# A spectral filter and the feed-forward block that gates it, on one core: one interleaved order of emission, statistics on two engines, filter rows gathered late

## The chip, the cores and the metric

One NeuronCore of one Trainium2 chip. The metric is the device time of one execution in microseconds (us), as the median of several executions. All runs here are of programs on one core; a run counts as "slow" when it is over 1.5% above the fastest run of the same kernel, and comparisons use the others alone.

Engines are named as the profile names them: PE is TensorE's matmul unit (PEld its weight loads), DVE is VectorE, ACT is ScalarE, POOL is GpSimd, SP is SyncE. A "q" behind the name (ACTq, SPq) marks the engine's own work of issuing DMAs. The "granted clock" is the share of PE's full clock that the profile records as let through. Its record starts only with PE's first dense work; for earlier windows the views print 1.00 without a record.

## The reference, cut to what matters

```python
def reference(A_x, A_w_r, A_w_i, B_x, B_w_gate, B_w_up, B_w_down):
    x  = A_x                                   # (1, 2048, 640) bf16
    xn = layernorm(x)                          # over the 640 columns, eps 1e-5
    s  = irfft2(rfft2(xn) * (w_r + 1j*w_i))    # over 2048 x 640; the filter has 2048 x 321 entries
    g  = silu((gelu(xn @ w_gate) * (xn @ w_up)) @ w_down)      # 640 -> 1536 -> 640
    return x + s * g
```

The two branches, spectral filter and feed-forward, need only `xn` and meet only in the last line. Both Fourier transforms are done as matmuls with constant tables.

## The kernel before

The kernel cuts the 2048 rows into 16 slabs of 128 and emits its work in blocks: loads and all 32 gathers of filter rows; statistics, normalisation and first Fourier stage ("fold") of all slabs; the whole spectral chain for eight groups G; then, for each of four groups of slabs, 12 gate/up steps followed by four times (inverse transform, down projection, result). The framework's scheduler can take later instructions forward, as far as buffers allow. The parts that matter, with cuts marked:

```python
    for G in range(8):                                   # 32 gathers, first thing on GpSimd
        for pm in range(2):
            for ri, wsrc in enumerate((A_w_r, A_w_i)):
                nc.gpsimd.indirect_dma_start(out=Wt[:, G, pm, ri, 0:L], ...)
    # ... loads of BD, Wd, I1T, IM, IT on GpSimd as well

    for b in range(4):
        for j in range(4):                               # statistics: VectorE only
            # ... bn_stats twice, bn_aggr -> mva[:, j]
        nc.gpsimd.tensor_scalar_add(out=ve, in0=mva[:, :, 1], scalar1=1e-5)
        nc.gpsimd.tensor_tensor(out=rstd, in0=ve, in1=mh, op=ALU.pow)
        for j in range(4):
            nc.vector.tensor_scalar(out=xn, in0=X[:, n1, :], scalar1=mva[:, j, 0:1], scalar2=rstd[:, j:j + 1], ...)
            nc.sync.dma_start(out=xnD[n1 * P:(n1 + 1) * P, :], in_=xn)             # to DRAM ...
            nc.sync.dma_start_transpose(out=xnT[...], in_=xnD[...])                # ... and back, transposed
        for j in range(4):                               # fold
            # ... eo, xf on VectorE; pa on TensorE
            A = work.tile([P, D], BF16, tag="s4", name=f"A{n1}", bufs=3)
            nc.scalar.copy(out=A, in_=flat(pa)[:, 0:D])
            nc.sync.dma_start(out=D2[:, n1, :], in_=A)   # regrouping goes through DRAM
    for q in range(4):
        nc.sync.dma_start(out=Bv[:, 4 * q:4 * q + 4, :], in_=D2[...])

    for G in range(8):                                   # the spectral chain
        # ... pzt (for every fourth G), pz -> Z -> pe -> E -> V -> M, N, Y, R (VectorE) -> pi -> IU
        nc.sync.dma_start(out=D3[G]..., in_=IU...)
    # ... reload of D3 into Uv

    for grp in range(4):                                 # feed-forward and inverse
        for t in range(12):
            # ... pg (5 matmuls), pu (5 matmuls), ge = gelu(pg) on ScalarE
            u = work.tile([P, 512], BF16, tag="uT", name=f"uT{grp}_{t}", bufs=14)
            nc.vector.tensor_tensor(out=u, in0=pu, in1=ge, op=ALU.mult)
        for j in range(4):
            y = inverse(n1)                              # pv, Vt, py, ... needs the whole chain
            # ... ph (24 matmuls), tanh, gating, result
```

## Time and profile before

| | before |
|---|---|
| median time (three runs) | 347.28 us |
| span of the profiled run | 345.6 us |
| PE busy | 224.3 us (65%) |
| first gate/up matmul (`pg`) | 60.7 us |
| spectral chain on PE, first `pzt` to last `pi` | 96.8 to 185.5 us |
| first inverse (`pv`) / first down projection (`ph`) | 193.5 / 196.2 us |

The first lines come from the page of the kernel before: busy time by engine, then the busy share in 40 equal slices of the span, in tenths (each slice is 8.6 us here).

```profile
PE 224.3 (65%) x1328; PEld 124.5 (36%) x1328; DVE 154.1 (45%) x366; ACT 101.1 (29%) x148; POOL 41.2 (12%) x50
...
PE   0000012958589983644352587999999999999873
...
POOL 6777791000000000000000000000000000000000
PEclk9999999998969998766665589999999999999999
```

PE is dense only from slice 26 on. It does next to nothing for seven slices, is patchy to slice 12, and patchy again, at a lower granted clock, from slice 16 to 24. The windows of the same run give these stretches in numbers (columns: window, its length, then for each engine busy us with the number of instructions; last the granted clock of PE, the DMA share and GB/s):

```profile
0.00:52.00 52.00, 1.21 (x4) 0.46 (x4) 18.42 (x65) 1.98 (x2) 40.42 (x50) 1.00 0.83 271
52.00:100.00 48.00, 30.35 (x130) 12.85 (x129) 22.41 (x73) 16.96 (x26) 0.77 (x1) 0.91 0.75 209
...
125.00:195.00 70.00, 30.93 (x184) 18.08 (x181) 30.02 (x54) 21.08 (x26) 0.00 (x0) 0.70 0.15 55
195.00:343.00 148.00, 138.04 (x875) 80.81 (x875) 68.65 (x146) 49.67 (x79) 0.00 (x0) 0.98 0.12 38
```

Two stretches lose the most: 52 us at the start with 1.2 us of PE work, and 70 us in the middle with 30.9. What happens in the first is in the timeline of the kernel before (start, duration, engine, instruction; in brackets the idle time of that engine just before, and what ended it):

```profile
24.64 0.21 DVE L234 BATCH_NORM_AGGREGATE mva_406<-stats_419 128x2 f32<-128x12 f32 x1
...
42.13 0.95 POOL L214 DMA_INDIRECT Wt<-in_A_w_i_dram,LANE  x1 [0.30 <-issue]
...
46.67 1.09 POOL L238 TENSOR_TENSOR rstd_169<-ve_168,mh 128x4 f32<-128x4 f32 x1
...
47.80 0.45 DVE L243 TENSOR_SCALAR xn_172<-X,mva_151,rstd_169 128x640 bf16<-128x640 bf16 x1 [22.95 <-POOL rstd_169 L238]
```

VectorE has all statistics at 24.9 us. GpSimd is still issuing gathers, one every 1.25 us, the last at 42.1, and computes the first `rstd` only at 46.7. VectorE stands still for 22.95 us. PE's waits show this and what the middle stretch waits for:

```profile
PE pa_194 L259 <- DVE xf_191 L256: 50.5, 1, 50.5
PE pv_1161 L355 <- DMA BU<-D_93: 8.1, 1, 8.1
PE pg_0_967 L388 <- DMA xnT<-xnD: 6.5, 1, 6.5
...
PE pi_0_785 L337 <- DVE R_781 L326: 5.1, 1, 5.1
```

A line like the last one comes for five of the eight G: PE gives VectorE the spectrum and waits 4.9 to 5.1 us for the filtered one (`R`). In that stretch there is no feed-forward work to put in: the next down projection stands behind an inverse that needs the whole chain, and the gate/up steps have used the 14 `u` buffers.

### The profile page before, as it was taken

How to read it: one execution, taken by the hardware profiler on the slowest of the kernel's cores; microseconds unless marked ns; L12 is line 12 of the kernel's file. 1: busy time of each engine (PE TensorE's matmuls, PEld its weight loads, DVE VectorE, ACT ScalarE, POOL GpSimd, SP SyncE). 2: the span in 40 equal slices, each digit the busy share in tenths (PEclk: the TensorE clock that was granted, in tenths of full speed). 3: DMA queues.
4: the chain of work that ended last, by engine and by line, in shares of the span. 5: the costliest groups of instructions: out<-in, count | busy, mean ns of one | idle time of the engine just before them, and what ended most of it. 6: DMA issues, size and time to landing. Idle time of an engine off the chain costs nothing. (4 is left out here: it accounts for less than half of the span.)

```text
span 345.6 us, 3623 instructions
## 1 busy us (share of the span) xinstructions
PE 224.3 (65%) x1328; PEld 124.5 (36%) x1328; DVE 154.1 (45%) x366; ACT 101.1 (29%) x148; POOL 41.2 (12%) x50
## 2 busy tenths in 40 slices
PE   0000012958589983644352587999999999999873
PEld 0000000423244442322231355546654466544652
DVE  2580046583207644354533136634563345633453
ACT  0000003433233553422330124233422334223341
POOL 6777791000000000000000000000000000000000
PEclk9999999998969998766665589999999999999999
DMA  7999286778570111101111811200220001200011
GB/s 268 372 339 310 67 269 174 226 218 193 142 275 1 41 38 38 39 4 35 38 38 38 307 38 38 78 0 22 57 78 0 1 23 55 65 13 0 21 39 38
DMA packets 33745, 34.85 MB, mean 101 GB/s; under 512 B 13168, under 2 KB 31344, under 8 KB 33600
## 3 DMA queue, kind: packets, MB, share of 16 engines
q1 hardware_dynamic: 25840, 23.67, 21.9%
q0 software_dynamic: 2208, 6.01, 5.3%
q10 hardware_dynamic: 5680, 4.95, 4.7%
q8 instruction: 10, 0.16, 0.2%
q14 instruction: 7, 0.06, 0.1%
HBM read 21.50 MB, written 10.50 MB: 93 GB/s over the span
## 5 line engine op out<-in xcount | busy, mean ns | idle before, releaser
L388 PEld LDWEIGHTS <-Wg 128*128 128x128 bf16 x240 | 23.4, 100 | 33.1 <-issue 8.7
L391 PEld LDWEIGHTS <-Wu 128*128 128x128 bf16 x240 | 23.9, 101 | 28.1 <-issue 3.5
L259 PE MATMUL pa_194<-xf_191,F1T 128*128 128x512 bf16 x1 | 0.6, 584 | 50.5 <-DVE xf_191 L256 50.5
L337 PEld LDWEIGHTS <-BD 128*128 128x128 bf16 x64 | 7.3, 124 | 35.0 <-DVE R_781 L326 5.3
L260 PEld LDWEIGHTS <-F1T 128*128 128x128 bf16 x16 | 1.7, 104 | 44.3 <-issue 43.9
L214 POOL DMA_INDIRECT Wt<-in_A_w_r_dram,LANE x16 | 15.2, 952 | 5.8 <-issue 4.6
L214 POOL DMA_INDIRECT Wt<-in_A_w_i_dram,LANE x16 | 15.1, 946 | 4.9 <-issue 4.9
L243 DVE TENSOR_SCALAR xn_172<-X,mva_151,rstd_169 128x640 bf16<-128x640 bf16 x1 | 0.4, 446 | 22.9 <-POOL rstd_169 L238 22.9
L262 ACT ACT_TABLE_LOAD x1 | 1.3, 1283 | 25.5 <-DMA Wu<-in_B_w_up_dram 25.5
L355 PEld LDWEIGHTS <-BU 128*128 128x128 bf16 x64 | 5.0, 100 | 10.3 <-DMA BU<-D_93 8.7
L259 PEld LDWEIGHTS <-F1T 128*128 128x128 bf16 x16 | 1.7, 108 | 18.1 <-DMA F1T<-tab_f 12.0
L262 ACT CAST A_197<-pa_194 128x640 bf16<-128x640 f32 x1 | 0.7, 692 | 24.5 <-PE pa_194 L260 24.5
L289 PEld LDWEIGHTS <-BU 128*128 128x128 bf16 x64 | 5.9, 125 | 2.3 <-issue 1.3
L388 PE MATMUL pg_0_967<-xnT,Wg 128*128 128x512 bf16 x5 | 2.3, 625 | 6.5 <-DMA xnT<-xnD 6.5
L355 PE MATMUL pv_1161<-I1T,BU 128*128 128x128 bf16 x4 | 0.6, 308 | 8.1 <-DMA BU<-D_93 8.1
L396 DVE TENSOR_TENSOR uT_8_1109<-pu_8_1096,ge_8_1107 128x512 bf16<-128x512 f32 x1 | 0.7, 692 | 10.0 <-PE pu_8_1096 L391 10.0
L374 DVE TENSOR_TENSOR y_1179<-y_1177 128x320 bf16<-128x320 bf16 x1 | 0.3, 326 | 10.9 <-ACT y_1177 L371 10.9
L280 PE MATMUL pzt_496<-T_77,BU 128*128 128x128 bf16 x8 | 1.2, 311 | 5.2 <-DMA BU<-D_92 5.2
L337 PE MATMUL pi_0_895<-R_891,BD 128*128 128x322 bf16 x4 | 1.3, 469 | 5.1 <-DVE R_891 L326 5.1
L337 PE MATMUL pi_0_785<-R_781,BD 128*128 128x322 bf16 x4 | 1.3, 468 | 5.1 <-DVE R_781 L326 5.1
L337 PE MATMUL pi_0_950<-R_946,BD 128*128 128x322 bf16 x4 | 1.3, 468 | 5.1 <-DVE R_946 L326 5.1
L337 PE MATMUL pi_0_719<-R_715,BD 128*128 128x322 bf16 x4 | 1.3, 469 | 5.0 <-DVE R_715 L326 5.0
(1054 smaller groups left out, 633.5 us busy)
## 6 DMA issues: line engine op xcount, KB each, us to landing
BU<-D_93 SPq DMA_DIRECT2D x4, 644.0 KB, 6.0
BU<-D_92 SPq DMA_DIRECT2D x4, 640.0 KB, 6.2
Wg<-in_B_w_gate_dram ACTq DMA_DIRECT2D x4, 480.0 KB, 15.0
Wu<-in_B_w_up_dram ACTq DMA_DIRECT2D x4, 480.0 KB, 13.0
X<-in_A_x_dram SPq DMA_DIRECT2D x3, 640.0 KB, 11.6
Wd<-in_B_w_down_dram POOLq DMA_DIRECT2D x1, 1920.0 KB, 9.1
BD<-tab_bd POOLq DMA_DIRECT2D x1, 1024.0 KB, 9.3
X<-in_A_x_dram SPq DMA_DIRECT2D x2, 320.0 KB, 6.8
```

What stands on the lines that cost most here:

```text
L214: nc.gpsimd.indirect_dma_start(out=Wt[:, G, pm, ri, 0:L], out_offset=None, in_=wsrc, in_offset=bass.IndirectOffsetOnAxis(ap=LANE[:, 2 * G ...
L243: nc.vector.tensor_scalar(out=xn, in0=X[:, n1, :], scalar1=mva[:, j, 0:1], scalar2=rstd[:, j:j + 1], op0=ALU.subtract, op1=ALU.mult)
L259: nc.tensor.matmul(pa[:, 0, :], lhsT=F1T, rhs=xf[:, :, 0:128], start=True, stop=True)
L260: nc.tensor.matmul(pa[:, 1, 0:128], lhsT=F1T, rhs=xf[:, :, 128:160], start=True, stop=True)
L262: nc.scalar.copy(out=A, in_=flat(pa)[:, 0:D])
L280: nc.tensor.matmul(pzv[:, i, :, h, :], lhsT=Bv[:, g, 512:640], rhs=T2[:, g, :], start=True, stop=True, skip_group_check=True)
L289: nc.tensor.matmul(pzv[:, c, :, h, :], lhsT=Bv[:, g, c * P:c * P + P], rhs=T2[:, g, :], start=True, stop=True, skip_group_check=True)
L337: nc.tensor.matmul(pi[:, pq, 0:LP], lhsT=BD[:, G, ro, ri, :], rhs=R[:, ri, pq, :], start=(ri == 0), stop=(ri == 1))
L355: nc.tensor.matmul(pvf[:, c * P:c * P + P], lhsT=U[:, cols[c]], rhs=I1T, start=True, stop=True, skip_group_check=True)
L388: nc.tensor.matmul(pg, lhsT=Wg[:, c, t * P:(t + 1) * P], rhs=xnT[:, c, q0:q0 + 512], start=(c == 0), stop=(c == 4))
L391: nc.tensor.matmul(pu, lhsT=Wu[:, c, t * P:(t + 1) * P], rhs=xnT[:, c, q0:q0 + 512], start=(c == 0), stop=(c == 4))
L396: nc.vector.tensor_tensor(out=u, in0=pu, in1=ge, op=ALU.mult)
```

## The change

Its intent: the work is emitted in one list of 64 feed-forward steps (48 gate/up steps, 16 down projections), and each piece of the rest is hung behind one step, so the spectral chain always has feed-forward matmuls between its pieces. A down projection no longer stands behind an inverse; nine `G2` buffers hold its result, and `u` has 16 buffers instead of 14. Statistics go to VectorE for one slab in three and to ScalarE for two; the transposed `xn` comes from PE for the first four slabs and by DMA straight from SBUF for the rest; the gathers are spread; the table of activation functions is loaded at the start.

```diff
-    for G in range(8):
-        ... 32 gathers, then BD, Wd, I1T, IM, IT on GpSimd
+    nc.scalar.activation(out=warm, in_=warm, func=ACT.Gelu_apprx_tanh)      # table load first
     ... X on SyncE (six pieces instead of five)
     for q in range(4):
         nc.scalar.dma_start(out=Wg[:, :, cs], in_=gv[:, :, cs])
         nc.scalar.dma_start(out=Wu[:, :, cs], in_=uv[:, :, cs])
+    nc.scalar.dma_start(out=Wd, ...)
+    for t, k in ((T2, "t2"), (FM, "fm"), (FT, "ft"), (BD, "bd"), (I1T, "i1"), (IM, "im"), (IT, "it")):
+        nc.scalar.dma_start(out=flat(t), in_=tabs[k])
...
+    def norm(n1):
+        if n1 % 3 == 0:
+            ... bn_stats, bn_aggr on VectorE, + eps on GpSimd
+        else:
+            nc.scalar.activation(out=junk, in_=x, func=ACT.Copy, scale=-1.0 / D, accum_out=nm)
+            nc.scalar.activation(out=junk, in_=x, func=ACT.Square, bias=nm, accum_out=ss)
+            ... mean, variance + eps on GpSimd
+        nc.gpsimd.tensor_tensor(out=rstd, in0=rstd, in1=mh, op=ALU.pow)
+        ... xn on VectorE
+        if n1 < 4:
+            ... five nc.tensor.transpose, then nc.scalar.copy(out=xnT[...], in_=pt)
+        else:
+            nc.sync.dma_start_transpose(out=xnT[:, :, n1 * P:(n1 + 1) * P], in_=xn)
...
+    def gather(G):
+        W = buf("W", "W", 4, (P, 2, 2, LP))
...
+    ffn = []
+    for grp in range(4):
+        ffn += [(gate_up, grp, t) for t in range(12)] + [(down, 4 * grp + j) for j in range(4)]
+    after = {i: [] for i in range(64)}
+    for i in range(12):
+        after[i].append((norm, 4 + i))
+        ... fold(nf), four of them for every three steps
+        if i in (5, 7, 9, 11):
+            after[i].append((gather, (i - 5) // 2))
+    after[11].append((regroup,))
+    for G in range(8):
+        i = 14 + 2 * G
+        after[i].append((spectral_a, G))
+        after[i + 1].append((spectral_b, G))
+        if G < 4:
+            after[i + 1].append((gather, G + 4))
+    after[29].append((reload,))
+    ... inverse(n1) at 32 + 2 * n1, final(n1) one step later
+    for i, (fn, *a) in enumerate(ffn):
+        fn(*a)
+        for f2, *b in after[i]:
+            f2(*b)
```

## The prediction

> **What bounds the kernel now.** TensorE, but only for part of the span: busy 224.3 of 345.6 us (page, part 1). Three stretches waste it.
>
> 1. 0 to 50.5 us: nothing on PE but a weight load (timeline). VectorE has its statistics by 24.9 us, then waits 22.9 us for rstd (costliest groups), because GpSimd first issues 32 filter gathers at 1.25 us each, up to 43 us. The first gate/up matmul starts only at 60.7 us, behind the xnD round trip through DRAM.
> 2. 52 to 100 us: PE is 15.7 of 28, then 14.6 of 20 us busy (windows).
> 3. 125 to 195 us: PE 30.9 of 70 us, granted clock 0.70. The feed-forward order has run out: 14 u buffers, and the first down projection stands behind the inverse. The spectral chain runs alone, about 10.7 us per G (pz to pz at 142.2, 153.4, 164.1), with 5.1 us of PE waiting for R each time.
>
> From 195 us on PE is dense (138 of 148 us, clock 0.98), so little can be gained there.
>
> **What the change does.** Statistics of slabs 1, 2, 4, 5... go to ScalarE (two passes of about 0.7 us, an estimate from the 128x640 casts); gathers of later G come late; the first four slabs are transposed on PE (20 small matmuls), the other twelve by DMA straight from SBUF, so the xnD write and wait go. Down projections no longer wait for the spectral chain: the instruction order puts about 26 feed-forward matmuls into each G. The table load moves to the start.
>
> **Costs, in order.**
> - ScalarE now issues 16 DMAs before its first computation, and the last one waits for the last Wu chunk. Before, all of X and W had landed by about 27 us; I count 8.4 MB ahead of it at about 340 GB/s, so ScalarE is free at about 25 us. "DMA: Bandwidth & Descriptors" of the Trainium skill (Issuing engines are not separate DMA queues) says queues share the same 16 engines; the trace agrees (DMA share 0.99 in 0 to 30 us). GpSimd still has 16 gathers in front, to about 24 us. Then statistics of slabs 1 and 2, pow (1.1 us), xn, transposes, copies: first gate/up matmul at about 33 us (was 60.7).
> - Group 0 (12 gate/up, 12 norms, 16 folds): 30 us of warm PE work, but VectorE and ScalarE each have about 31 us in it too: about 40 us.
> - The whole matmul order is 197 us at 2.4 GHz (estimate: columns/2.4 plus 2.5 ns, "TensorE: Matmul & The Clock Gate", Wait; the trace has 1.08 us for 5x512, which agrees).
> - Spectral stretch: chain 9.7 to 10.7 us per G against 8.9 us of PE: about 8 us of stalls. Reload: 8 us against 7 us of fill.
> - Later bubbles 4 us, tail 5 us.
>
> 33 + 196 + 10 + 8 + 1 + 4 + 5 = about 258 us. Some 27 us come from the start, the rest from filling 125 to 195 us.
>
> **Signs.** First gate/up at 30 to 36 us; no 22.9 us rstd wait; one table load; PE over 80% busy at clock near 1.0 from 80 us on; waits for R under 2 us; PE total about 225 us or less.
>
> **What would make it wrong.** SBUF-sourced DMA transposes could occupy the SP queue far longer than the 1.21 us of the DRAM-sourced ones; D2 stores queue behind them and everything slides. ScalarE freed later than 25 us. GpSimd's small operations (1.6 us per slab) or shared buffers serialising group 0. Then 280 us or more.
>
> Predicted 258 us, 8 in 10 between 243 and 284. Faster 0.95, same 0.02, slower 0.03.

## The result, and the profile after

The changed kernel takes 262.26 us (median of 4 runs, 261.18 to 263.19) against 347.41 us for the kernel before in the same rounds. The ratio is 0.7551, with a 95% interval from 0.7509 to 0.7593. Ratios here and below are the mean time of one kernel's fast runs over the mean of the other's fast runs of the same rounds, so they are not quite the ratio of the medians quoted.

The page of the kernel after (a slice is 6.5 us now):

```profile
PE 208.8 (80%) x1348; PEld 118.2 (45%) x1348; DVE 144.5 (56%) x337; ACT 117.5 (45%) x192; POOL 50.2 (19%) x87
...
PE   0010079999999999999999877779999999999881
```

PE has 15.5 us less busy time than before although it has 20 matmuls more (its mean granted clock is 0.995 against 0.914), and it is dense from slice 7 on; slices 23 to 27 are the only soft spot. The windows, cut at the stages:

```profile
0.00:36.00 36.00, 2.91 (x21) 2.03 (x22) 10.49 (x33) 8.78 (x18) 21.33 (x38) 1.00 1.01 333
36.00:68.00 32.00, 31.63 (x150) 14.26 (x149) 25.03 (x79) 26.92 (x56) 12.88 (x30) 1.00 0.61 165
68.00:78.00 10.00, 10.00 (x75) 7.16 (x74) 2.33 (x3) 2.10 (x3) 0.00 (x0) 1.00 0.62 211
78.00:166.00 88.00, 79.34 (x515) 43.85 (x514) 53.56 (x97) 41.92 (x57) 15.95 (x20) 1.00 0.17 51
166.00:174.00 8.00, 6.59 (x50) 4.44 (x48) 3.09 (x5) 2.60 (x4) 0.00 (x0) 1.00 0.55 185
174.00:255.00 81.00, 78.32 (x546) 46.43 (x543) 48.22 (x119) 35.14 (x55) 0.00 (x0) 1.00 0.23 76
```

The spectral chain (78 to 166 us) takes about as long as before (87.3 us, 88.7 before), but PE is now busy 79.3 of its 88 us at full clock. Of 51.1 us without PE work (259.9 less 208.8), 33.1 lie in the first 36 us. The timeline of the kernel after shows the start:

```profile
27.31 0.95 POOL L282 DMA_INDIRECT W<-in_A_w_i_dram,LANE  x1 [0.30 <-issue]
28.11 0.69 ACT L245 COPY xnT<-pt 128x640 bf16<-128x640 bf16 x1 [25.37 <-issue]
...
31.45 0.45 DVE L240 TENSOR_SCALAR xn<-X,mean,rstd 128x640 bf16<-128x640 bf16 x1 [15.48 <-POOL rstd L238]
```

Only half of "gathered late" came about: the pool `W` has four buffers, so the scheduler took the first 16 gathers forward to 7.5 to 28.3 us, and only the other 16 are late. ScalarE does its first work on data at 28.1 us, 25.4 us after the small activation that brings the table load, because it was issuing loads: 17.0 of the 25.4 us are issues, the rest lies between them. VectorE still waits for `rstd`, 15.5 us in the last line, now because ScalarE's statistics come late. PE's waits after, to be held against those of before:

```profile
PE pt L244 <- DVE xn L240: 32.6, 3, 17.9
PE pi L356 <- DVE R L345: 5.8, 7, 1.9
```

Seven waits for `R` add up to 5.8 us; before, the eight added up to 28.2.

### The profile page after: what moved, and what is told of

It is laid out like the page before. It is cut to its first block, busy times and chain, and to the rows that moved or that the text cites. A ratio compares the mean times of both kernels' runs of the same rounds, so it can differ in the third digit from the quotient of the medians.

```text
span 259.9 us, 3724 instructions
## 1 busy us (share of the span) xinstructions
PE 208.8 (80%) x1348; PEld 118.2 (45%) x1348; DVE 144.5 (56%) x337; ACT 117.5 (45%) x192; POOL 50.2 (19%) x87
## 5 line engine op out<-in xcount | busy, mean ns | idle before, releaser
L409 PE MATMUL pg<-xnT,Wg 128*128 128x512 bf16 x240 | 63.5, 384 | 0.0
L411 PE MATMUL pu<-xnT,Wu 128*128 128x512 bf16 x240 | 62.2, 380 | 0.0
L423 PE MATMUL ph<-Wd,u 128*128 128x320 bf16 x384 | 53.9, 299 | 1.0 <-ACT E L324 0.6
L423 PEld LDWEIGHTS <-u 128*128 128x128 bf16 x384 | 37.4, 98 | 16.1 <-issue 1.6
L415 DVE TENSOR_TENSOR u<-pu,ge 128x512 bf16<-128x512 f32 x48 | 32.9, 686 | 20.9 <-PE pu L411 17.1
L413 ACT ACTIVATE ge<-pg 128x512 bf16<-128x512 f32 x48 | 28.9, 602 | 18.6 <-PE pg L409 16.1
L426 ACT ACTIVATE th<-ph 128x640 f32<-128x640 f32 x16 | 11.3, 704 | 42.6 <-PE ph L423 42.6
L282 POOL DMA_INDIRECT W<-in_A_w_r_dram,LANE x16 | 15.4, 965 | 11.0 <-DMA LANE<-tab_lane 5.3
L282 POOL DMA_INDIRECT W<-in_A_w_i_dram,LANE x16 | 15.4, 965 | 4.8 <-issue 4.8
L356 PE MATMUL pi<-R,BD 128*128 128x322 bf16 x64 | 10.8, 301 | 6.4 <-DVE R L345 5.8
L324 ACT CAST E<-pe 128x644 bf16<-128x644 f32 x16 | 13.1, 888 | 4.6 <-PE pe L322 4.6
L240 DVE TENSOR_SCALAR xn<-X,mean,rstd 128x640 bf16<-128x640 bf16 x10 | 4.4, 443 | 18.4 <-POOL rstd L238 18.2
L245 ACT COPY xnT<-pt 128x640 bf16<-128x640 bf16 x4 | 2.6, 687 | 25.8 <-issue 25.4
L263 ACT CAST A<-pa 128x640 bf16<-128x640 f32 x16 | 10.9, 697 | 4.3 <-DMA D_92<-A 2.6
L327 DVE TENSOR_TENSOR V<-E 128x644 bf16<-128x644 bf16 x8 | 4.0, 495 | 13.4 <-ACT E L324 13.3
## 6 DMA issues: line engine op xcount, KB each, us to landing
Wg<-in_B_w_gate_dram ACTq DMA_DIRECT2D x4, 480.0 KB, 10.9
```

Source lines behind the costliest of these rows:

```text
L282: nc.gpsimd.indirect_dma_start(out=W[:, pm, ri, 0:L], out_offset=None, in_=wsrc, in_offset=bass.IndirectOffsetOnAxis(ap=LANE[:, 2 * G + pm ...
L324: nc.scalar.copy(out=E[:, ri].rearrange("p r (i q) -> p r q i", q=2), in_=pe[:, :, 0:LP].rearrange("p r (q i) -> p r q i", q=2))
L356: nc.tensor.matmul(pi[:, pq, 0:LP], lhsT=BD[:, G, ro, ri, :], rhs=R[:, ri, pq, :], start=(ri == 0), stop=(ri == 1))
L409: nc.tensor.matmul(pg, lhsT=Wg[:, c, t * P:(t + 1) * P], rhs=xnT[:, c, cols], start=(c == 0), stop=(c == 4))
L411: nc.tensor.matmul(pu, lhsT=Wu[:, c, t * P:(t + 1) * P], rhs=xnT[:, c, cols], start=(c == 0), stop=(c == 4))
L413: nc.scalar.activation(out=ge, in_=pg, func=ACT.Gelu_apprx_tanh)
```

## The experiments

Twelve kernels were run; all gave correct results. Their ratios are against the kernel before, run on the same chip in the same rounds (medians of before 346.58 to 347.24 us). All had three rounds, the last two named (`c3`, `d1`) five. Kernels of different groups (`b`, `a1`, `a4`, `a8`; the other `a`; `c`; `d`) ran on different chips, so small differences between groups are not read. "First `pg`", "folds end" (last `pa`) and "chain starts" (first `pzt`) are times on PE; "chain lasts" runs to the last `pi`, "rest" from there to the end of the span. All five are from the profiled run, which for `a8` is the slow one; the three fast runs of `a8` took 267.75 to 271.47 us.

| run | median us | ratio to before | first `pg` | folds end | chain starts | chain lasts | rest |
|---|---|---|---|---|---|---|---|
| before | 347.41 | | 60.7 | 82.5 | 96.8 | 88.7 | 160.1 |
| after | 262.26 | 0.755 | 36.4 | 68.5 | 78.1 | 87.3 | 94.5 |
| b1_gathers_behind_rstd | 333.56 | 0.962 | 43.3 | 68.1 | 82.9 | 88.9 | 159.7 |
| a1_chain_in_one_block | 303.74 | 0.878 | 36.2 | 67.9 | 74.9 | 87.1 | 139.4 |
| a4_gathers_behind_norms | 259.40 | 0.749 | 33.4 | 65.5 | 75.1 | 87.9 | 93.9 |
| a8_stats_one_engine | 270.50 | 0.778 | 48.5 | 79.6 | 89.2 | 88.9 | 93.9 |
| a3_loads_off_scalar | 268.77 | 0.774 | 20.5 | 65.3 | 77.8 | 95.0 | 94.0 |
| a5_both | 264.67 | 0.764 | 14.5 | 62.9 | 77.2 | 90.5 | 94.6 |
| a6_start_rebuilt | 270.60 | 0.779 | 14.1 | 62.3 | 75.5 | 99.3 | 94.5 |
| a9_stats_one_engine | 278.94 | 0.803 | 13.6 | 68.2 | 89.7 | 93.7 | 94.2 |
| c1_nine_a_buffers | 256.28 | 0.739 | 14.6 | 50.8 | 66.0 | 93.8 | 94.0 |
| c2_chain_eight_steps_later | 251.58 | 0.724 | 14.8 | 59.6 | 81.4 | 93.3 | 76.6 |
| c3_later_chain_nine_buffers | 246.46 | 0.711 | 15.0 | 50.7 | 75.0 | 93.3 | 75.9 |
| d1_inverses_one_step_later | 253.49 | 0.731 | 14.4 | 50.1 | 84.5 | 93.3 | 72.3 |

The last three columns add up to the span, about 2 us less than the time. The chain lasts 87 to 99 us in every order; what changes most is the rest behind it: 160 us in the order of before, 139 in `a1`, 94 to 95 in the order of the kernel after, 72 to 77 where the chain comes eight steps later. Of the 85.7 us of span between before and after, 18.7 are the chain's earlier start, 1.4 the chain, and 65.6 the shorter rest.

### Is it the start? The gathers moved alone, in the kernel before

The first question is how the 85 us divide. In the kernel before, only the gathers move: they are held back until the last `rstd` has been issued (`issue_after` holds what is emitted inside it behind the instruction given).

```diff
-    for G in range(8): ... 32 gathers
...
-        nc.gpsimd.tensor_tensor(out=rstd, in0=ve, in1=mh, op=ALU.pow)
+        last_pow = nc.gpsimd.tensor_tensor(out=rstd, in0=ve, in1=mh, op=ALU.pow)
...
+    with tc.issue_after(last_pow.ins):
+        for G in range(8): ... 32 gathers
```

> The kernel before, with one thing changed: the 32 filter gathers are queued on GpSimd behind the last rstd. If the 22.9 us wait for rstd is really on the path, the first gate/up matmul comes about 20 us earlier (40 us instead of 60.7) and nearly all of that is kept, since the spectral chain hangs on the folds: about 327 us. Rival: DMA traffic and the SP queue hold the folds back anyway, then less than 5 us is won (342 us or more).

Measured: 333.56 us, ratio 0.962 (0.956 to 0.968). Time fell, by less than expected. The folds end 14.4 us earlier, and 13.0 us of that are kept in the time. But the middle stretch is as it was; its window in this run, taken 14 us earlier because the chain starts that much earlier:

```profile
111.00:181.00 70.00, 31.56 (x182) 18.48 (x180) 30.02 (x54) 20.61 (x26) 0.00 (x0) 0.67 0.14 51
```

So the gathers in front of `rstd` explain some 13 us, and not the middle.

### Is it the order? The chain put back in one block, in the kernel after

```diff
     for G in range(8):
-        i = 14 + 2 * G
-        after[i].append((spectral_a, G))
-        after[i + 1].append((spectral_b, G))
+        after[11].append((spectral_a, G))
+        after[11].append((spectral_b, G))
         if G < 4:
-            after[i + 1].append((gather, G + 4))
-    after[29].append((reload,))
+            after[11].append((gather, G + 4))
+    after[11].append((reload,))
```

> The changed kernel, with the interleave undone: all eight spectral steps and the reload are emitted in one block straight after the regroup; start, statistics and gathers stay as changed. If the fill of the spectral stretch is worth what I said, TensorE runs out of feed-forward work after about 4 gate/up steps, the chain runs alone at 10.5 to 11 us per G at a lowered clock, and the time is about 303 us (plus 40). Rival: the chain of 10 us per G sets the length of the stretch in both orders and the fill is merely moved, then under 270 us.

Measured: 303.74 us, ratio 0.878 (0.873 to 0.882), very close to what was expected. Start, statistics, transposes and table load are those of the kernel after; the interleaving alone is worth 41.5 us (303.74 less 262.26). Between before and `a1` lie 44.2 us of span: the chain starts 21.9 us earlier, and the rest behind it is 20.7 us shorter. How these divide among the moved gathers, the transposes, the split statistics and the down projections freed from the inverse, no run shows. Its stretch from 78 to 166 us, and its waits for `R` there:

```profile
78.00:166.00 88.00, 49.36 (x284) 29.10 (x283) 41.88 (x78) 28.72 (x36) 15.78 (x20) 0.75 0.17 52
```

```profile
PE pi L356 <- DVE R L345: 34.7, 7, 5.1
```

In the same 88 us the kernel after has 79.3 us of PE work and 5.8 us of these waits. The waits for `R` shrank although VectorE has the same work for each G; PE now has something to do during them. The Trainium skill ("TensorE: Matmul & The Clock Gate", Part 1: The HAM clock gate) says that PE's clock falls to half after an idle window of about 3.4 us. The trace agrees in kind: with gaps of 5 us the granted clock of this stretch is 0.75, with gaps below 2 us it is 1.00, and the half-clock spells recorded in this stretch of `a1` are 3.4 or 6.8 us long. After such a gap eight `pi` matmuls of `a1` start 0.27 us apart, against 0.14 in the kernel after. So a gap costs twice, by itself and by the slower matmuls after it.

### The first 36 us: gathers and loads

In the kernel after, two things could hold the first gate/up matmul at 36.4 us: the 16 early gathers, and ScalarE's 16 load issues in front of its first computation. Each was removed alone, then both.

```diff
 # a4_gathers_behind_norms
-        if i in (5, 7, 9, 11):
-            after[i].append((gather, (i - 5) // 2))
-    after[11].append((regroup,))
+    after[11] += [(gather, G) for G in range(4)] + [(regroup,)]
 # and in gather(G):
+        with tc.issue_after(pow_of[15].ins):        # pow of the last norm
             ... memset and four gathers
 # a3_loads_off_scalar: the 16 loads of ScalarE are issued by SyncE
-        nc.scalar.dma_start(...)
+        nc.sync.dma_start(...)
 # a5_both: both edits
```

> The changed kernel with the first 16 gathers, which the instruction order had put at 7.5 to 28.3 us, queued behind the last norm on GpSimd. Theory: the start waits for ScalarE (busy issuing DMAs to 28.1 us) as much as for GpSimd, so freeing GpSimd alone gains at most 2 us (260 to 263 us). Rival: GpSimd is what holds the start, then about 10 us is won.

> The changed kernel with the 16 loads that ScalarE issues moved to the SP queue; gathers stay in front. Theory of two limits in parallel: GpSimd, still issuing gathers to about 28 us, holds rstd of slabs 1 and 2, so the first gate/up matmul moves from 36.4 to 32 us at best, 258 to 262 us. Rival: ScalarE alone holds the start; then about 245 us.

> Both at once: loads on the SP queue and the first 16 gathers behind the last norm. If two limits stand in parallel, the gain is far larger than the sum of the single ones (3 us for the gathers alone): first gate/up matmul at 15 to 20 us, 243 to 250 us. Rival: a third limit, the loads themselves (8.4 MB at about 340 GB/s, or SP issuing loads while the D2 stores wait), holds the start; then 254 us or more.

Measured: `a4` 259.40 us (ratio 0.749, 0.745 to 0.753), 1.1% below the kernel after by the medians; the two intervals overlap (0.751 to 0.753) and the rounds differ, so this small gain rests also on the profiled spans, 256.9 against 259.9 us. Its timeline has the copy that was at 28.11 us:

```profile
25.18 0.69 ACT L245 COPY xnT<-pt 128x640 bf16<-128x640 bf16 x1 [22.43 <-issue]
```

ScalarE is free 2.9 us earlier although none of its own instructions changed. The Trainium skill ("DMA: Bandwidth & Descriptors", Issuing engines are not separate DMA queues) says that DMAs of all engines run on the same 16 DMA engines and interleave. That agrees: the gathers carry about 1.3 MB (16 gathers of 128 rows of 642 bytes), which at the 333 GB/s of that window is an estimated 3.9 us of transfer, and ScalarE's issues end earlier without them (the longest takes 3.8 us instead of 4.8). The 2.9 us reach the end: so much is also 262.26 less 259.40.

`a3` and `a5` were misses. The first gate/up matmul came at 20.5 and 14.5 us, earlier than expected, but the times were 268.77 and 264.67 us, above the kernel after. Starting the feed-forward 22 us earlier gained nothing: the table shows the chain starting at 77 to 78 us in all three. An early feed-forward start alone is not on the critical path. It even cost something: the rest behind the chain is 94 to 95 us as in the kernel after, and the chain itself lasts 95.0 and 90.5 us instead of 87.3, with waits for `R` of up to 5.1 us again, since matmuls done before the chain are no longer there to fill it (258 and 240 feed-forward matmuls lie in it, instead of 269).

A further kernel (`a6`) orders the loads by need: X and gate/up weights alternate on SyncE, the eight later loads go to GpSimd behind the `pow` of slab 7, the gathers behind that of slab 15.

```diff
     for a, b in ((0, 1), (1, 2), (2, 4), (4, 8), (8, 12), (12, 16)):
         nc.sync.dma_start(out=X[:, a:b, :], in_=xv[:, a:b, :])
+        ... behind pieces 3 to 6: one quarter each of Wg and Wu, on nc.sync
-    nc.scalar.dma_start(out=Wd, ...); T2, FM, FT, BD, I1T, IM, IT
+    def late_loads():                                  # emitted after step 3
+        with tc.issue_after(pow_of[7].ins):
+            ... the same eight loads on nc.gpsimd
```

> A candidate to beat both kernels: X and the gate/up weights interleaved on the SP queue, the eight later loads on GpSimd behind the eighth norm, gathers behind the last norm. First gate/up matmul at about 15 us, group 0 as before about 32 us if its engines keep pace, 240 to 247 us. If the loads or GpSimd's extra issues slow group 0, 250 us or more.

Measured: 270.60 us (ratio 0.779, 0.776 to 0.782), a miss as well. It shows one place where the early start is given back, in the windows and in the timeline:

```profile
36.00:45.00 9.00, 0.50 (x3) 0.17 (x2) 0.17 (x1) 2.00 (x4) 0.00 (x0) 0.72 0.93 339
```

```profile
43.00 1.29 ACT L261 CAST A<-pa 128x640 bf16<-128x640 f32 x2 [11.70 <-DMA D<-A]
```

For 9 us the DMA engines move 339 GB/s, mostly late loads, and ScalarE waits 11.7 us for one of three `A` buffers, whose store to DRAM stands among them. It is not the only place: ScalarE also has two waits, 16.2 us together, whose releaser the profile doesn't name (more under "One step more"). The wait for `A` gave the theory that the next runs test.

### The statistics on one engine

```diff
-        if n1 % 3 == 0:
+        if True:                       # all statistics on VectorE
```

> The changed kernel with all statistics on VectorE. VectorE gets 10 more slabs of about 1.1 us, ScalarE loses 10 of about 1.9 us. If the split over two engines pays, group 0 becomes longer by 5 us or more (267 us or more). Rival: the split costs as much as it gives, because the statistics of slabs 1 and 2 wait on ScalarE until 28 us while VectorE sits idle; then the same or up to 3 us faster (259 to 263 us).

> The candidate with all statistics on VectorE, a clean test of the split, since ScalarE no longer starts late: VectorE gets 10 slabs of about 1.1 us more inside group 0, ScalarE 10 of about 1.9 us less. If the split pays, 5 us or more slower than the candidate; rival: ScalarE was as full as VectorE in group 0 (26.9 of 32 us against 25.0), so the same within 2 us.

In the kernel after (`a8`), it took 270.50 us (267.75 to 271.47 in the fast runs), but the test is confounded, and its profile is of a slow run: in that run ScalarE's last load issues slipped (to 45.2 us, from 27.4 in the kernel after), its first copy came at 45.7 us, and the first gate/up matmul at 48.5. So it was repeated on `a6`, where ScalarE issues no loads: `a9` took 278.94 us against 270.60, 8.3 us more, with the folds ending at 68.2 instead of 62.3 us. So the split over two engines seems to pay there. The size is not clean either: `a9` has one wait of 14.8 us that the profile can't put down to anything, `a6` two of 16.2 together. Its worth in the kernel after itself was not measured cleanly.

### Two theories of what fixes the start of the chain

Theory A: the early start is given back because the copies into `A` wait for stores to land; more `A` buffers would end the folds earlier. Theory B: the chain cannot start before about 77 us, so an early start pays only if there is more feed-forward work in front of the chain. Theory C, the rival of B: the total is the chain's start, the chain and what follows, so work moved in front of the chain will be missing later as fill. All three edits are made to `a5` (264.67 us). So as to take no more SBUF, `A` borrows the nine `G2` buffers, which nothing uses before the first down projection.

```diff
 # c1_nine_a_buffers
-        A = buf("A", "s4", 3)
+        A = flat(buf("A", "G2", 9, (P, 2, 320)))
 # c2_chain_eight_steps_later
-        i = 14 + 2 * G
+        i = 22 + 2 * G
-    after[29].append((reload,))
+    after[37].append((reload,))
-    ... inverse(n1) at 32 + 2 * n1, final one step later
+    for n1 in range(16):
+        i = 43 + n1 * 21 // 16
+        after[i].append((inverse, n1))
+        if n1 < 12:
+            after[i + 1].append((final, n1))
 # c3_later_chain_nine_buffers: both
```

> The early-start kernel a5 (264.7 us) with the A tiles of the folds taken from the nine G2 buffers, which nothing uses yet, instead of three. Theory A (the early start was given back because the copies to A wait for the D2 stores to land): ScalarE's waits of A on the DMA (3.5 us and an unexplained 7.6 us in a5) go, the folds end by about 57 us (was 62.9), the first pzt comes at 68 to 70 us (was 77.2), and the time falls to about 256. Theory B (the transfers themselves, and nothing else, set when the regrouped data arrive): the folds may end a little earlier but pzt stays at 75 to 77 us and the time within 2 us of 264.7.

> a5 with the whole spectral chain moved eight feed-forward steps later in the order (22 + 2G in place of 14 + 2G; inverses from step 43), A buffers as they were. Theory B (start of the chain is fixed at about 77 us, so an early feed-forward start pays only if there is enough feed-forward work in front of the chain): eight steps are 18.4 us of warm PE work; the first pzt comes at 77 to 84 us without a wait of more than 2 us, and the time falls from 264.7 to 246 to 252. Theory C (total is set by the chain's start plus the chain plus what follows it): the time does not fall, or rises, because work moved in front of the chain is missing as fill later; 262 to 270.

> Both: chain eight steps later and nine A buffers, on a5. If B is right, 243 to 250 us, the fastest of all; PE busy over 90% of 20 to 235 us. If only A is right, about 256, as c1. If C is right, 258 or more.

Measured: `c1` 256.28 us (ratio 0.739, 0.736 to 0.742), `c2` 251.58 (0.724, 0.722 to 0.726), `c3` 246.46 (0.711, 0.708 to 0.713). Against `a5` these are 8.4, 13.1 and 18.2 us less. But `a5`, on another chip, has one wait that none of the three has ("remote" is a releaser that the profile can't name):

```profile
ACT A L263 <- remote: 7.6, 1, 7.6
```

So the sizes are better read from the three alone, which ran in the same rounds: nine buffers give 5.1 us (`c2` less `c3`), the later chain 9.8 (`c1` less `c3`). Losing the unnamed wait would be the other 3.3 of the 18.2, an estimate by difference. A and B both hold. B's claim that the buffers would not move the chain's start is wrong (66.0 us in `c1`). C's forecast for `c2` (262 to 270) failed, although its sum holds in every row of the table: in `c2` the rest behind the chain fell from 94.6 us to 76.6, since fewer steps of the list stand behind it, while the chain grew only from 90.5 to 93.3. What C describes is rather what happened to `a3` and `a5`. ScalarE's waits from 14 to 66 us show A. First `c2`, which has three `A` buffers:

```profile
ACT A L263 <- DMA D<-A: 8.2, 4, 3.5
```

In `c1`, with nine, no wait of this kind is left; the only DMA wait of `A` is this:

```profile
ACT A L263 <- DMA xnT<-xn: 0.7, 1, 0.7
```

And `c3` in windows:

```profile
36.00:56.00 20.00, 19.92 (x112) 10.05 (x111) 12.55 (x37) 8.93 (x14) 12.20 (x17) 1.00 0.98 201
56.00:78.00 22.00, 21.99 (x140) 12.46 (x138) 6.52 (x9) 7.36 (x11) 6.81 (x8) 1.00 0.75 226
78.00:100.00 22.00, 20.91 (x123) 10.46 (x120) 14.92 (x30) 10.30 (x15) 7.54 (x10) 1.00 0.15 40
```

PE has hardly a gap between the end of the folds (50.7 us) and the chain (75.0 us), in which the folded data go out to DRAM and come back. From 78 to 166 us PE is busy 84.4 of 88 us (20.9 and three later windows of 19.2, 19.0 and 25.4), more than in the kernel after: the later steps of the list fill the chain as well as the earlier ones did.

`c3` is the fastest kernel. The ratio of its ratio to that of the kernel after (0.711 by 0.755) is 0.94, so it is about 6% faster; the two did not run in the same rounds.

### One step more

In `c3`, the longest wait of PE after the start is for the reload in front of the first inverse. Its waits and those of a kernel with the inverses one step later:

```diff
-        i = 43 + n1 * 21 // 16
+        i = 44 + n1 * 20 // 16
         after[i].append((inverse, n1))
         if n1 < 12:
-            after[i + 1].append((final, n1))
+            after[i].append((final, n1))
```

> The fastest so far (later chain and nine A buffers, 246.46 us) with the inverses from step 44 in place of 43, so that one down projection (24 matmuls, 3.3 us) stands between the chain's last matmul and the first inverse. There TensorE waits 5.2 us for the reload of the filtered data with only 3.2 us of work in front of it. If that wait is on the critical path it shrinks to about 2 us and the time falls to 243 to 244.5; if what follows (copies of ScalarE in the last stretch) bounds the end, the time stays within 1 us of 246.5.

```profile
PE pv L376 <- DMA BU<-D: 5.2, 1, 5.2
```

```profile
PE pv L376 <- DMA BU<-D: 1.7, 1, 1.7
```

The wait shrank as expected (first `c3`, then `d1`), but `d1` took 253.49 us (ratio 0.731, 0.729 to 0.733), 7 us more than `c3`. The rest behind the chain did get shorter, 72.3 us instead of 75.9. The time went where nothing was edited: the chain starts at 84.5 us instead of 75.0. The window of `d1` against the one of `c3` above, two of its PE lines and one of ScalarE:

```profile
56.00:78.00 22.00, 15.94 (x76) 7.87 (x75) 3.75 (x5) 3.31 (x5) 6.49 (x7) 0.77 0.69 213
```

```profile
61.13 0.44 PE L424 MATMUL ph<-Wd,u 128*128 128x320 bf16 x1 [1.11 <-issue]
63.21 0.42 PE L424 MATMUL ph<-Wd,u 128*128 128x320 bf16 x1 [1.64 <-issue]
...
66.83 0.70 ACT L427 ACTIVATE th<-ph 128x640 f32<-128x640 f32 x1 [12.03 <-remote]
```

From 58 to 67 us PE gives out single matmuls with gaps that the profile puts down to nothing ("issue"), and ScalarE has a wait of 12 us that it puts down to nothing it can name either ("remote"). Yet the lists of instructions of `c3` and `d1` are the same on every engine up to a point far behind this stretch. All five runs of `d1` lie between 252.26 and 254.26 us, so this belongs to the program and not to a single run. Similar waits are in `a5` (7.6 us for `A`), `a6` (two for `th`, 7.7 and 8.6 us) and `a9` (one for `th`, 14.8 us). What they wait for was not found. Full DMA engines are not enough: from 58 to 67 us their share is 1.03 in `d1` and 0.97 in `c3`, which has no such wait. Another candidate is the fetch of instructions, which is a DMA of its own; the page of `d1` lists it:

```profile
q8 instruction: 10, 0.16, 0.3%
```

The page of `c3` has the same line, and the packed trace of `d1` speaks against it: the fetched blocks land at 54.3 and 58.2 us and the next at 83.6, so none lands where the wait ends, at 66.8 us. The cause stays open.

## Why the prediction was right, point by point

The time (262.26 against 258, range 243 to 284) and the direction were right, and so was the mechanism, a middle stretch filled with feed-forward work. That the total came so close is in part luck: errors of several us in its terms cancel. In the table, the first measured column takes PE's busy time from the windows of the kernel after. The second counts each matmul as the prediction did (columns over 2.4 GHz plus 2.5 ns), an estimate worked out over the 1348 matmuls of the trace; all other time is then a stall.

| term | predicted us | measured, by busy time | measured, by matmul work |
|---|---|---|---|
| start, to the first gate/up matmul | 33 | 36.0 (cut of the window) | 36.0 |
| stalls in group 0 | 10 | 0.4 | 2.0 |
| stalls between group 0 and chain | none | 0.0 | 0.2 |
| stalls in the spectral stretch | 8 | 8.7 (88 less 79.3) | 13.3 |
| reload beyond its fill | 1 | 1.4 | 1.6 |
| later bubbles | 4 | 2.7 (81 less 78.3) | 5.8 |
| tail | 5 | 4.9 (259.9 less 255) | 4.9 |
| PE work from group 0 on | 196 | 205.9 (208.8 less 2.9) | 196.1 |

- **What bounded the kernel before: right in kind.** `b1` moved the gathers alone and got 13 us, `a1` has everything but the interleaving and is 41.5 us slower than the kernel after. The prediction gave 27 us to the start and the rest (some 62) to filling 125 to 195 us; by the table of runs the chain starts 18.7 us earlier and 65.6 us are saved behind it. So the order holds, but interleaving accounts for 41.5 us and not 62. One claim failed: "From 195 us on PE is dense, so little can be gained there". From the first inverse on, 19.9 us were not matmul work before and 10.8 after, by the same estimate.
- **"First gate/up matmul at about 33 us": 3 us off, and the step that failed is known.** The prediction put ScalarE free "at about 25 us", behind "8.4 MB ahead of it", and did not charge the 16 gathers that it had itself placed in front, to about 24 us. They share the DMA engines. ScalarE was free at 28.1 us; in `a4`, without these gathers, at 25.2 us with the first `pg` at 33.4, the predicted figures.
- **"Group 0 ... about 40 us": wrong by 8.** It took 31.9 us (36.4 to 68.3), and the "30 us of warm PE work" was right (30.0 by matmul work). The step that failed: VectorE's and ScalarE's 31 us each were taken to add to PE's. They were busy 25.0 and 26.9 of the 32 us, beside PE and not before it.
- **"The whole matmul order is 197 us": right as work.** The trace gives 197.4 by the rule from the Trainium skill ("TensorE: Matmul & The Clock Gate", Wait — 56ns, not 53.3ns?: columns over 2.4 GHz plus 2.5 ns), which the trace agrees with: it makes 1.08 us of five matmuls of 512 columns, and the next five start 1.08 us later. Busy time is 208.8 us because the same five show 1.24 us: a matmul's end runs past the next one's start, so short stalls are counted as busy (4.4 us in front of the 25 gaps, 7.0 elsewhere).
- **Spectral stretch: the stalls were forecast 5 us too small.** "Chain 9.7 to 10.7 us per G against 8.9 us of PE" measured 10.9 against 9.3. With the start (3 us) and the later bubbles (2 us) this offsets the error in group 0. Reload and tail were right within 1 us. The sign "waits for R under 2 us" held: the longest was 1.9.
- **Signs.** One table load, at 1.24 us; no 22.9 us wait for `rstd`, though one of 15.5 is left; clock 1.00 in every window from 36 us on. The first five gate/up matmuls still took 2.29 us, twice the 1.08 of later ones. A first gate/up matmul at 36.4 us is just past the predicted 30 to 36. "PE over 80% busy from 80 us on" held on average (90% from 78 to 166 us), but not for the end of that stretch, where four slices show 7 tenths. PE's total of 208.8 us is below the 225 named.
- **The fear that DMA transposes from SBUF would be slow: not borne out.** SyncE's issues of them were 1.2 to 1.3 us each but for one of 1.6, against mostly 1.21 us for those from DRAM.
- **What the prediction did not see.** It measured the start by the first gate/up matmul alone. `a3`, `a5` and `a6` show that this is not enough: behind the first gate/up matmul stood a second limit, the stores of `A` and the regrouping through DRAM, and freeing the start paid only with more `A` buffers (`c1`), more feed-forward work in front of the chain (`c2`), or both (`c3`).

## What to carry to other kernels

When two branches share an engine and one is a chain with waits of several microseconds, emit them as one list with a step of the independent branch between the pieces of the chain; here that was worth 41.5 of 85 us, and the clock came back with it. When a start is made earlier and the time doesn't move, split the time at the chain: its start, its length, and the rest behind it. Here the start stayed at 75 to 78 us in `a3` to `a6`, until the `A` buffers were widened, and the rest shrank only when more steps of the list came before the chain's end. And hold a bulk transfer that isn't needed yet behind the last instruction that others wait for: the gathers were worth 13 us in `b1`, 2.9 in `a4` and 4.1 between `a3` and `a5`. But don't hold it into a stretch whose stores need the same DMA engines, as the late loads of `a6` did.

## What the Trainium skill lacked or had wrong

- "DMA: Bandwidth & Descriptors", Issuing engines are not separate DMA queues: it says that issuing from several engines saves only sequencer time, which is usually small. It gives no size for an issue while the DMA engines are full, where it was not small for an engine that also computes: in the kernel after, ScalarE's first copy came 25.4 us after its first activation, and single issues of the 16 took up to 4.8 us there and 3.8 in `a4` (the short ones 0.4 to 0.7 us). Its main statement agrees with the traces (2.9 us for ScalarE from taking away GpSimd's gathers).
- "ScalarE: Activation LUTs", What ACT_TABLE_LOAD costs: it gives about 1283 ns for the load and about 1380 ns more for a drain at every switch. The load took 1.28 us here, but for the first load of the program no drain is seen behind it: in `a4` it ran from 1.25 to 2.53 us and the next activation started at 2.54. No run here switches between tables.
- "Runtime: NRT & Kernel Launch", Instruction fetch mechanics: it says that fetch comes in 16 KiB blocks by a DMA queue of its own and that its cost is mostly hidden. The trace agrees for the queue q8 (10 packets of 16 KiB, 0.16 MB). It has a second queue of the kind "instruction", q14, with 7 packets of 8 KiB (0.06 MB), which the page lacks.
- No page read here tells what the profile's "remote" wait stands for; it was up to 14.8 us long (`a9`), and its cause stays open.
